# Attention values with the exp blocks as weights: V and a column of ones moving through TensorE, x turned back by transposes

## The chip, the cores and the metric

One NeuronCore of a Trainium2 chip runs the whole program. The metric is device time in microseconds (us), taken several times; the median counts. The profile is one further execution, with the start and end of every instruction. The engines are PE (TensorE; its weight loads are listed apart as PEld), ACT (ScalarE), DVE (VectorE), POOL (GpSimd) and SP, which only issues DMAs.

## The reference

Attention over 8 batches of 12 heads, 448 positions and 64 channels, with q and k normalised, and a two-layer product on its result:

```python
q_n, k_n = rmsnorm(q, g_q), rmsnorm(k, g_k)           # x / sqrt(mean(x*x) + 1e-6) * g
scores = matmul(q_n, k_n.T) / sqrt(64)                # per batch and head, 448 x 448
attn = exp(scores - max);  attn = attn / (sum(attn) + 1e-9)
x = matmul(attn, v)                                   # heads side by side: 3584 x 768
h = x @ w_in                                          # 768 -> 2048
g = h + sin(alpha * h)**2 / (alpha + 1e-9)
out = g @ w_out                                       # 2048 -> 768
```

The inputs are float32; matmul operands are bf16, sums are float32 in PSUM.

## The kernel before

**Stages.** The work goes batch by batch, in eight stages, b = 0 to 7. In stage b the kernel makes the attention of batch b (12 heads, in three groups c = 0, 1, 2 of four heads) and the first product of batch b. The second product of batch b-1 is cut into units of 64 matmuls and pushed in small steps of 8 matmuls between the attention's steps of stage b. After stage 7 the second product of batch 7 stands alone: the tail.

**The order is written out by hand.** Each stage has a string of tokens (`STAGE_0` for b = 0, `STAGE_1` for b = 1, `STAGE_N` for all later ones), which the program walks from left to right; each engine's queue holds what its tokens issued, in that order. A digit n stands for n steps `F` of the second product's oldest unit, `f` is a step of the next unit (`fill`, of lines L548 and L529). `S` is one tile of scores: four matmuls (L357) and one exp on ACT (L360) for four heads, 64 keys each, and 448 queries. `o`, `v`, `x`, `y`, `z` are parts of `attend`: the sums of the exps by matmuls with ones (L404, L416) and the values product (L416), with V as the weights and the exps moving. `q`, `u`, `r`, `g`, `k` are the normalisation of q and k: squares (L281 on POOL, L278 on ACT), their sums on DVE (L290), the inverse root on ACT (L299, L300), the product with g on POOL (L286) and the scaling (L309, on POOL, or on DVE in stage 0). `t` turns the result by a DMA transpose that SP issues (L319), `p` by TensorE (L334). `l`, `V`, `W`, `O` load q and k (SP), v, w_in and w_out (POOL).

**The values product before.** A tile of exps holds keys in partitions and queries along the row, so x comes out with channels in partitions, which is what the first product wants. The division is made in three ways on ACT and DVE: the sums' logarithm and exp(-ln) on ACT (L423 to L432), for group 0 folded by four reductions on DVE (L429), and then a product out of PSUM on DVE into xT (L440).

**The first product** (`first_product`, L468) has 96 matmuls of 128 x 128 weights and 448 columns a stage. Two matmuls' outputs share a PSUM pair; each pair goes through sin on ACT (L446), a square on POOL (L449) or ACT (L451) and a sum on DVE (L454) into g_sb. It starts on the groups of x that are ready.

**PSUM** is four slots of two banks. Which slot each step takes is a written string of digits too; a step waits until the last reader of its slot is done.

Of the kernel before, what the change touches and what calls it, by code (L numbers as in the profile page):

```python
# [17 lines left out]
try:  # L18
# [15 lines left out]
        "q000 u000 q010 G q011 q001 u010 g00 u011 r01 g01 D1 u001 k01 r00 k00 q11 u11 O00 q10 V00 p012 "  # L34
        "W01 q20 p00 g1 u10 r1 q21 u20 V01 g2 S4 V02 S k11 l3 k10 S1 S1 S4 W00 W02 S u21 r2 p1 L S2 S q31 "
        "S3 k21 q30 k20 D2 S S3 o3 l4 g3 S W10 W12 o1 o3 p2 u30 l5 S3 u31 S1 S W11 S4 v7 S S S q40 S S x5 "
        "y3 q41 u41 x1 g4 z4 u40 x1 r4 y4 O01 q50 z3 r3 O10 "
    ),
    "012311203203312021021302301231032103021321302",
    {-1: 'u50 O11 k30', 0: 'D4 k401', 1: 'k411', 2: 'q51', 3: 'k31 k400 u51', 5: 'k410', 7: 'g5 V12', 8: 't3 V10 V11 t4 l6 l7'},  # L40
# [3 lines left out]
        "4 r2 f f k20 1 f f 2 k21 S 1 q31 1 t2 S 1 S 2 S q30 2 S 2 S S 3 f S 3 S 1 f S 1 S 1 u31 2 l5 g3 "  # L44
        "S u30 o1 o6 1 r3 V10 2 S f q41 1 f 2 S 2 S 2 q40 S u41 1 v1 v1 S v3 V12 S k31 q50 v2 u40 S 2 S "
        "V11 g5 S z4 x7 y7 r4 z3 g4 k30 "
    ),
    "1320201203203013133213130101301231203123",
    {-1: 'u50 t3', 0: 'k41', 2: 'k40', 5: 'q51', 6: 'l6 t4', 8: 'u51 l7'},
# [3 lines left out]
        "f q40 f 1 f 2 q41 1 S 1 r2 5 f S f f S 2 S 1 u40 k20 1 k21 S 1 u41 1 S 2 S 1 q31 1 o7 1 f f 1 S "  # L53
        "t2 f 1 r4 S 2 f 1 l5 q30 S 3 S 1 u31 1 S 2 u30 g3 V10 S 2 S S k41 3 S v6 r3 k30 S k31 v1 S 2 V12 "
        "g4 2 S 2 S 2 q51 l6 S t3 z3 x7 y5 y2 z4 V11 "
    ),
    "01223131310312323203013012301021310231023",
    {-1: 'k40', 0: 't4', 2: 'q50', 3: 'u50', 4: 'u51 g5', 6: 'l7'},
)
LAST = "0123012"  # L60


def tokens_of(plan):

    return [t for word in plan.split() for t in ("F" * int(word) if word.isdigit() else [word])]
# [3 lines left out]
def kernel(  # L69
# [14 lines left out]

# [12 lines left out]
    NC = NP // 2  # L105
    SCALE = float(D) ** -0.5
# [8 lines left out]
    vpool = ctx.enter_context(tc.tile_pool(name="vpool", bufs=2))  # L115
    npool = ctx.enter_context(tc.tile_pool(name="norm", bufs=2))
    tpool = ctx.enter_context(tc.tile_pool(name="qkT", bufs=8))
    epool = ctx.enter_context(tc.tile_pool(name="expT", bufs=17))
    hpool = ctx.enter_context(tc.tile_pool(name="parts", bufs=1))
    rpool = ctx.enter_context(tc.tile_pool(name="rec", bufs=2))  # L120
    xpool = ctx.enter_context(tc.tile_pool(name="xT", bufs=1))
# [6 lines left out]

# [3 lines left out]
    upcoming = deque()  # L132
# [11 lines left out]
    qk, vb, norm = {}, {}, {}  # L144

    def strip(pp, hi):

        s = 2 * hi + pp
        return slice(s * 32, s * 32 + 32)

    def half_of(c, pp, hi):

        return pp ^ (hi, 1, 0)[c]

    def load_qk(ci, k_queue=nc.sync):

# [17 lines left out]
    def load_v(b, c):  # L174


        if b not in vb:
            vb[b] = vpool.tile([P, NP, NJ, D], BF16, tag="vb", name="vb")
        heads = v[b].rearrange("(n pp) (p j) d -> n pp p (j d)", pp=2, j=NJ)
        rows = vb[b].rearrange("p n j d -> p n (j d)")  # L180
        if c == 1:
            for r in range(2):
                nc.gpsimd.dma_start(out=rows[r * 64:r * 64 + 64, 1:4], in_=heads[1:4, 1 - r].rearrange("n p x -> p n x"))
        else:
            n = slice(0, 1) if c == 0 else slice(4, NP)
            nc.gpsimd.dma_start(out=rows[:, n], in_=heads[n].rearrange("n pp p x -> (pp p) n x"))
# [15 lines left out]
    ones = const.tile([P, D], BF16)  # L202
    nc.vector.memset(ones, 1.0)
    ones_row = const.tile([1, P], F32)
    nc.vector.memset(ones_row, 1.0)
    eps = const.tile([P, 1], F32)
# [13 lines left out]
    def spread_g():  # L220

        nc.gpsimd.tensor_mul(g_rows[:, 2], g_rows[:, 0], g_rows[:, 1])
        ps = bank_pair("gps")
        nc.tensor.matmul(ps[:, 0, :D], ones_row, g_rows[:, 2], start=True, stop=True)
        nc.vector.tensor_copy(gg[:, 0], ps[:, 0, :D])
        give_back(ps)

    def spread_alpha():

# [6 lines left out]
    def load_w_in(half, c):  # L236


        cols = slice(half * D_FF // 2, (half + 1) * D_FF // 2)
        rows = moe_w_in[c * 2 * P:(c + 1) * 2 * P, cols]  # L240
        nc.gpsimd.dma_start(out=w_in_sb[half][:, 2 * c:2 * c + 2],  # L241
                            in_=rows.rearrange("(p x) f -> p x f" if c else "(x p) f -> p x f", x=2))

    def load_w_out(hi, lo):
        src = moe_w_out.rearrange("(mt p) d -> p mt d", p=P)
        part = 2 * hi + lo
        mts = slice(part * MT // 4, (part + 1) * MT // 4)
        nc.gpsimd.dma_start(out=w_out_sb[:, mts], in_=src[:, mts])  # L248

    def keep_busy(n, rhs):  # L250


# [7 lines left out]
    def norm_tasks(ci):  # L260

        st = SimpleNamespace()
        early = ci <= NC
        st.ms = npool.tile([P, 2, 2 * NJ], F32, tag="ms", name="ms")
        st.inv, st.inv_ps, st.scaled = {}, [], 0
        st.sq, st.n = {}, None
# [5 lines left out]
        def square(w, heads=(0, 1)):  # L274
            if ci < 2:
                st.sq[w] = spare(2 * ci + w).rearrange("p (a d) -> p a d", d=D)
                rows = slice(heads[0] * NJ, (heads[-1] + 1) * NJ)
                nc.scalar.activation(st.sq[w][:, rows], qk[ci][:, w, rows], ACT.Square)  # L278
            else:
                st.sq[w] = npool.tile([P, 2 * NJ, D], F32, tag="sq", name="sq")  # L280
                nc.gpsimd.tensor_mul(st.sq[w], qk[ci][:, w], qk[ci][:, w])  # L281
# [10 lines left out]
        def rsqrt(ws=slice(0, 2)):  # L292
            ln = npool.tile([P, 2, 2 * NJ], F32, tag="inv", name="inv")
            inv = bank_pair("inv") if early else ln
            if early:
                st.inv_ps.append(inv)
            for w in range(2)[ws]:
                st.inv[w] = inv[:, w, :2 * NJ]
            nc.scalar.activation(ln[:, ws], st.ms[:, ws, :], ACT.Ln, scale=1.0 / D, bias=eps)  # L299
            nc.scalar.activation(inv[:, ws, :2 * NJ], ln[:, ws], ACT.Exp, scale=-0.5)  # L300

        def scale(w, heads=(0, 1)):
            eng = nc.vector if early else nc.gpsimd
# [20 lines left out]


# [22 lines left out]
    def scores(c, j, warm=0):  # L348

# [3 lines left out]
        for pp in range(2):  # L353
            for hi in range(2):
                qkt, r = qkT[2 * c + pp], slice(hi * 64, hi * 64 + 64)
                o = half_of(c % NC, pp, hi) * 64
                nc.tensor.matmul(sc[o:o + 64, hi, :S], qkt[r, 1, j * REST:(j + 1) * REST], qkt[r, 0, :],  # L357
# [5 lines left out]
    avs, recs = {}, {}  # L363
    presums = {}

    def add_tile(b):


        if b not in presums:
            presums[b] = SimpleNamespace(n=0, t=rpool.tile([P, 2, S], F32, tag="rec", name="rec"))  # L370
        s = presums[b]
        first = expT[b * NC, 0] if s.n == 0 else s.t
        s.n += 1
        nc.vector.tensor_add(s.t, first, expT[b * NC, s.n])

    def split_sum(b):

        s = presums[b]
        assert s.n == NJ - 1
        s.parts = [hpool.tile([P, 2, S], BF16, tag=f"part{i}", name="part") for i in range(2)]  # L380
        nc.vector.tensor_copy(s.parts[0], s.t)
        nc.vector.tensor_sub(s.parts[1], s.t, s.parts[0])
    STEPS = {"o": "ones 0", "v": "values 0", "x": "ones 1", "y": "low 1", "z": "high 1"}

    def attend(b, what, tiles=range(NJ)):

        kind, both = what.split()
        both = both == "1"  # L390
        if tiles[0] == 0:
            avs[what] = bank_pair("av")
        av = avs[what]
# [287 lines left out]
```

The softmax here doesn't subtract the row's maximum and nothing guards it: scores larger than these inputs give would overflow.

## Time and profile before

| what | value |
|---|---|
| time, median of 3 runs | 409.0 us (408.0 to 409.46) |
| span of the profiled execution, first to last instruction | 405.8 us |
| PE busy | 391.4 us (96%) |
| ACT busy | 315.3 us (78%) |
| POOL busy | 283.6 us (70%) |
| DVE busy | 240.6 us (59%) |
| granted TensorE clock | 0.999 of full |
| DMA, mean | 137 GB/s |

The page gives the span of the profiled execution and no other time of it; the median of the runs is 3.2 us longer than that span, which is what lies around it. The time in a row of a group is the union of its instructions' times; neighbouring matmuls overlap in the array, so a group's mean is longer than its share. "Idle before" is idle time of that engine, with what ended it.

### The profile page before, as it was taken

The numbers are of one execution on the slowest core, as the hardware profiler recorded it, in microseconds if no ns is written. First come the engines' busy times: TensorE is split into PE (matmuls) and PEld (weight loads), VectorE is DVE, ScalarE is ACT, GpSimd is POOL, SyncE is SP. The second block draws the span as 40 slices with busy tenths as digits, with TensorE's granted clock in tenths as the row PEclk, the third lists the DMA queues.
The fourth block names the chain that finished last, engine by engine and source line by source line (L and its number), as shares of the span: only waits on it lengthen the run. The fifth ranks groups of instructions, "written<-read, shape, count | busy, mean of one in ns | idle before, by whom it ended". The sixth has DMA issues, their size and how long they took to land.

```text
span 405.8 us, 15218 instructions
## 1 busy us (share of the span) xinstructions
PE 391.4 (96%) x6755; PEld 238.8 (59%) x6758; DVE 240.6 (59%) x364; ACT 315.3 (78%) x474; POOL 283.6 (70%) x268
## 2 busy tenths in 40 slices
PE   1999999999999999999999999999999999999996
PEld 1346467645675566755676556755667556765564
DVE  4956665756783576638584475836685485544512
ACT  5798889868896879958898678958898679877600
POOL 5998889987959789588877779597895784003300
PEclk9999999999999999999999999999999999999999
DMA  7999999855286925697076923879046901620022
GB/s 266 215 254 241 210 221 255 193 155 171 53 164 162 151 94 88 182 198 153 3 140 178 200 102 70 185 158 209 3 94 179 166 2 22 108 61 1 2 78 79
DMA packets 67846, 55.46 MB, mean 137 GB/s; under 512 B 41524, under 2 KB 63172, under 8 KB 67780
## 3 DMA queue, kind: packets, MB, share of 16 engines
q1 hardware_dynamic: 56578, 41.43, 42.2%
q0 software_dynamic: 10432, 11.81, 19.0%
q8 instruction: 53, 0.87, 0.9%
q10 hardware_dynamic: 770, 1.25, 0.9%
q14 instruction: 13, 0.11, 0.1%
HBM read 45.62 MB, written 11.01 MB: 140 GB/s over the span
## 4 chain that ended last, share of the span: by engine, by line
PE 88%; POOL 5%; DMA 3%; issue 1%; DVE 1%; ACT 1%; SPq 0%; POOLq 0%
PE hps L468 34%; PE ops L548 31%; PE av L416 9%; PE sc L357 7%; PE ops L529 5%; POOL sq L281 2%; DMA qk<-in_q_dram 2%; DMA qk<-in_k_dram 2%; PE av L404 1%; POOL qk L286 1%; POOL w_out_sb L248 1%; POOL w_in L241 1%; ACT expT L360 1%; DVE g_sb L454 0%; DVE xT L440 0%
## 5 line engine op out<-in xcount | busy, mean ns | idle before, releaser
L360 ACT ACTIVATE expT<-sc 128x896 bf16<-128x896 f32 x168 | 143.7, 917 | 7.4 <-PE sc L357 6.6
L548 PE MATMUL ops<-w_out_sb,g_sb 64*64 64x384 bf16 x3072 | 148.0, 323 | 0.0
L468 PE MATMUL hps<-xT,w_in 128*128 128x448 bf16 x768 | 147.0, 353 | 0.4 <-DVE g_sb L454 0.4
L468 PEld LDWEIGHTS <-w_in 128*128 128x128 bf16 x768 | 74.4, 98 | 72.5 <-issue 3.9
L454 DVE SCALAR_TENSOR_TENSOR g_sb<-s,inv_alpha_sb,hps 128x448 bf16<-128x448 f32 x128 | 81.1, 676 | 59.1 <-POOL s L449 58.5
L548 PEld LDWEIGHTS <-g_sb 64*64 64x64 bf16 x3072 | 91.9, 107 | 37.0 <-issue 3.8
L449 POOL TENSOR_TENSOR s<-s 128x448 f32<-128x448 f32 x64 | 59.6, 932 | 65.7 <-ACT s L446 43.9
L446 ACT ACTIVATE s<-hps,alpha_sb 128x448 f32<-128x448 f32 x128 | 73.9, 627 | 37.7 <-PE hps L468 37.2
L309 POOL TENSOR_TENSOR qkn<-qk,inv 128x448 bf16<-128x448 f32 x80 | 72.9, 938 | 24.6 <-issue 17.1
L281 POOL TENSOR_TENSOR sq<-qk 128x896 f32<-128x896 f32 x44 | 73.3, 1678 | 3.9 <-DVE ms L290 3.0
L357 PE MATMUL sc<-qkT 64*64 64x448 bf16 x672 | 60.3, 357 | 0.7 <-ACT expT L360 0.3
L286 POOL TENSOR_TENSOR qk<-qk,gg 128x896 f32<-128x896 f32 (+1 forms) x25 | 50.5, 2021 | 2.2 <-ACT g_sb L278 1.5
L554 DVE COPY osb<-ops 128x384 f32<-128x384 f32 x48 | 26.7, 556 | 38.5 <-PE ops L548 38.3
L290 DVE TENSOR_REDUCE ms<-sq 128x14 f32<-128x896 f32 x44 | 46.4, 1078 | 3.3 <-POOL sq L281 3.2
L440 DVE TENSOR_TENSOR xT<-av,rec 128x896 bf16<-128x896 f32 (+1 forms) x26 | 25.7, 1016 | 26.8 <-ACT rec L432 21.4
L451 ACT ACTIVATE s<-s 128x448 f32<-128x448 f32 x64 | 36.9, 577 | 2.9 <-DVE g_sb L454 0.7
L416 PE MATMUL av<-expT,vb 64*32 64x448 bf16 (+1 forms) x1120 | 38.1, 350 | 0.0
L357 PEld LDWEIGHTS <-qkT 64*64 64x64 bf16 x672 | 21.7, 107 | 13.8 <-issue 6.7
L555 DVE TENSOR_TENSOR osb<-osb,ops 128x384 f32<-128x384 f32 x48 | 26.6, 554 | 1.7
L416 PEld LDWEIGHTS <-vb 64*32 64x32 bf16 (+1 forms) x1120 | 20.8, 96 | 11.0 <-issue 2.2
L429 DVE TENSOR_REDUCE rec<-rec 32x448 f32<-32x448 f32 x28 | 17.1, 610 | 9.7 <-ACT rec L425 9.4
L529 PE MATMUL ops<-w_out_sb,g_sb 128*128 128x384 bf16 (+1 forms) x144 | 21.0, 309 | 0.0
(51 smaller groups left out, 185.8 us busy)
## 6 DMA issues: line engine op xcount, KB each, us to landing
qk<-in_q_dram SPq DMA_DIRECT2D x23, 448.0 KB, 5.2
qk<-in_k_dram SPq DMA_DIRECT2D x23, 448.0 KB, 5.7
out_dram<-osb SPq DMA_DIRECT2D x45, 192.0 KB, 2.9
w_out_sb<-in_moe_w_out_dram POOLq DMA_DIRECT2D x4, 768.0 KB, 12.8
w_in<-in_moe_w_in_dram POOLq DMA_DIRECT2D x6, 512.0 KB, 12.2
vb<-in_v_dram POOLq DMA_DIRECT2D x16, 168.0 KB, 7.2
vb<-in_v_dram POOLq DMA_DIRECT2D x8, 224.0 KB, 5.3
out_dram<-osb SPq DMA_DIRECT2D x13, 96.0 KB, 4.3
```

The source lines that it names most:

```text
L281: nc.gpsimd.tensor_mul(st.sq[w], qk[ci][:, w], qk[ci][:, w])
L286: nc.gpsimd.tensor_mul(x, x, gg.to_broadcast([P, len(heads) * NJ, D]))
L290: nc.vector.reduce_sum(st.ms[:, w, rows], st.sq[w][:, rows], axis=AX.X)
L309: eng.tensor_mul(n[:, :, hi, :], x[:, hi], inv[:, hi].unsqueeze(2).to_broadcast([P, NJ, D]))
L357: nc.tensor.matmul(sc[o:o + 64, hi, :S], qkt[r, 1, j * REST:(j + 1) * REST], qkt[r, 0, :], start=True, stop=True)
L360: nc.scalar.activation(expT[c, j], sc[:, :, :S], ACT.Exp, scale=SCALE)
L416: nc.tensor.matmul(av[o, k, :S], w, x[r, hi, :], start=(j == 0), stop=(j == last))
L446: nc.scalar.activation(s1, hps, ACT.Sin, scale=alpha_sb[:, m, :])
L449: nc.gpsimd.tensor_mul(s2, s1, s1)
L454: nc.vector.scalar_tensor_tensor(g_sb[:, m, (b % 2) * S:(b % 2 + 1) * S], s2, inv_alpha_sb[:, m, :], hps, op0=ALU.mult, op1=ALU.add)
L468: nc.tensor.matmul(ps[:, m % 2, :S], w_in_sb[m * 2 // MT][:, kt, m % (MT // 2) * P:(m % (MT // 2) + 1) * P], x[:, kt, :], start=(kt == ORD ...
L548: nc.tensor.matmul(st["ps"][os, r, :HALF], g_sb[rs, m, c0 + o * 64:c0 + o * 64 + 64], w_out_sb[rs, m, half * HALF:(half + 1) * HALF], star ...
```

## The change

V gets a column of ones, and swaps its place with the exps. A block of exps of 128 keys by 128 queries is the weights, and V's 64 channels with the ones (65 columns) move. Queries are now in the output's partitions, 65 columns for each block of 128 queries: 64 of x and one of the sum. The tiles of scores pair two key strips of one head in the 128 partitions; of the seven strips of 64 keys the last has no partner, and holds two heads. So for a group there are six paired tiles and one last one, and four heads of 448 queries give, in each paired tile, six blocks of 128 queries and two half blocks of 64, and in the last tile 28 quarter-array blocks.

DVE takes the reciprocal of the sums and multiplies (L378, L380); x then has queries in partitions, and is turned back: by a DMA transpose on SP (`T`, `turn`) or by seven matmuls and a copy (`P`, `pe_turn`: stage 0, and the last group of stage 1). V is loaded as float32 by SP, three loads a batch, and cast into v_pair and v_last by POOL (`c`) or DVE (`C`). Some squares move from POOL to ACT (`Q`), and the scaling after `R` is on POOL. The first product is opened early: `H` runs, for two outputs, the four of six steps that need only groups 0 and 1, inside the token string. The token strings and the slots are written anew; batch 0's second product takes all left halves first, each stored by itself.

```diff
 STAGE_N = (
     (
-        "f q40 f 1 f 2 q41 1 S 1 r2 5 f S f f S 2 S 1 u40 k20 1 k21 S 1 u41 1 S 2 S 1 q31 1 o7 1 f f 1 S "
-        "t2 f 1 r4 S 2 f 1 l5 q30 S 3 S 1 u31 1 S 2 u30 g3 V10 S 2 S S k41 3 S v6 r3 k30 S k31 v1 S 2 V12 "
-        "g4 2 S 2 S 2 q51 l6 S t3 z3 x7 y5 y2 z4 V11 "
+        "3 q40 S 1 g4 f 2 f f S 2 S 2 S u40 3 S R2 V10 2 S q30 1 S 2 S 2 q41 V11 S k20 1 v6 v1 S f f S f f S "
+        "S f S k21 V12 u41 f t2 f 1 f 1 R4 u30 T0 k41 l5 2 S 1 S S k40 3 v6 Q31 S v1 2 S 2 S 2 u31 Q50 f 1 S "
+        "v7 r3 f f c12 g3 T1 f f f T2 3 H u50 k30 Q51 g5 k31 H C10 C11 u51 l7 t3 l6 t4 "
     ),
...
-    epool = ctx.enter_context(tc.tile_pool(name="expT", bufs=17))
+    epool = ctx.enter_context(tc.tile_pool(name="expT", bufs=14))
...
+    def load_v(b, part):
+        if b not in vs:
+            vs[b] = [vpool.tile([P, H, NK, D], F32, tag="vs", name="vs"), vpool.tile([P, NP, D], F32, tag="vl", name="vl")]
+        if part < 2:
+            rows = v[b].rearrange("h (p j) d -> p h j d", j=NJ)[:, :, part * NK:(part + 1) * NK]
+            nc.sync.dma_start(out=vs[b][0][part * 64:part * 64 + 64], in_=rows)
         else:
-            n = slice(0, 1) if c == 0 else slice(4, NP)
-            nc.gpsimd.dma_start(out=rows[:, n], in_=heads[n].rearrange("n pp p x -> (pp p) n x"))
+            rows = v[b].rearrange("(n pp) (p j) d -> pp p n j d", pp=2, j=NJ)[:, :, :, NJ - 1]
+            nc.sync.dma_start(out=vs[b][1], in_=rows.rearrange("pp p n d -> (pp p) n d"))
+
+    def cast_v(b, c, eng):
+        heads = slice(4 * c, 4 * c + 4)
+        eng.tensor_copy(v_pair[b % 2][:, heads, :, :D].rearrange("p h j d -> p (h j) d"),
+                        vs[b][0][:, heads].rearrange("p h j d -> p (h j) d"))
+        eng.tensor_copy(v_last[b % 2][:, 2 * c:2 * c + 2, :D], vs[b][1][:, 2 * c:2 * c + 2])
...
+    def values(b, c, js):
+        if js[0] == 0:
+            avs[b, c] = bank_pair("av")
+        av = avs[b, c]
+        es = {j: expT.pop((b * NC + c, j)).rearrange("p hi s -> p (hi s)") for j in js}
+        for whole in (True, False):
+            for j in js:
+                if j == NJ - 1:
+                    continue
+                pp, k = divmod(j, NK)
+                for i in range(NJ):
+                    if (i == NJ // 2) == whole:
+                        continue
+                    for o in range(1 if whole else 2):
+                        hi = o if i == NJ // 2 else i // (NJ // 2 + 1)
+                        n = P if whole else 64
+                        q0 = i * P + o * 64
+                        nc.tensor.matmul(av[o * 64:o * 64 + n, pp, i * W:(i + 1) * W], es[j][:, q0:q0 + n],
+                                         v_pair[b % 2][:, 4 * c + 2 * hi + pp, k], start=(k == 0 and i == 0), stop=False)
+        if js[-1] < NJ - 1:
             return
+        for i in range(NJ):
+            for o in range(2):
+                pos = 2 * i + o
                 for pp in range(2):
...
+                    r = slice(pp * 64, pp * 64 + 64)
+                    nc.tensor.matmul(av[o * 64:o * 64 + 64, pp, i * W:(i + 1) * W], es[NJ - 1][r, pos * 64:pos * 64 + 64],
+                                     v_last[b % 2][r, 2 * c + pos // NJ], start=False, stop=(i == NJ - 1))
+        sums = av[:, :, :NJ * W].rearrange("p pp (i w) -> p pp i w", w=W)
+        rec = npool.tile([P, 2, NJ, 1], F32, tag="rec", name="rec")
+        nc.vector.reciprocal(rec, sums[:, :, :, D:])
+        xn[b, c] = npool.tile([P, NJ, 2, D], BF16, tag="xn", name="xn")
+        nc.vector.tensor_mul(xn[b, c].rearrange("p i pp d -> p pp i d"), sums[:, :, :, :D], rec.to_broadcast([P, 2, NJ, D]))
+        give_back(avs.pop((b, c)))
+
+    def turn(b, c):
+        x = xT[b, c] = xpool.tile([P, 2, S], BF16, tag="xT", name="xT")
+        nc.sync.dma_start_transpose(out=x.rearrange("p k s -> p (k s)").rearrange("p (i t) -> p i t", t=P),
+                                    in_=xn.pop((b, c)).rearrange("p i pp d -> p (i pp d)"))
+
+    def pe_turn(b, c, act):
+        tp = bank_pair("xt", BF16)
+        src = xn.pop((b, c))
+        for i in range(NJ):
+            nc.tensor.transpose(tp[:, 0, i * P:(i + 1) * P], src[:, i].rearrange("p pp d -> p (pp d)"), ident)
+        x = xT[b, c] = xpool.tile([P, 2, S], BF16, tag="xT", name="xT")
+        out = x.rearrange("p k s -> p (k s)")
+        if act:
+            nc.scalar.copy(out, tp[:, 0, :2 * S])
         else:
...
+            nc.vector.tensor_copy(out, tp[:, 0, :2 * S])
+        give_back(tp)
...
+    def open_product(b):
+        i = len(opened)
+        opened[i] = bank_pair("hps")
+        for m in (2 * i, 2 * i + 1):
+            multiply(b, i, m, range(KT - 2))
```

`multiply` issues the first product's matmuls of one output (128 of the 2048 columns) for the given steps kt; `first_product` closes the opened outputs with the two steps of group 2 and goes on with the others. The end of stage 0's new string, which the prediction walks, is this:

```text
... q31 q30 v7 S S1 W12 u31 D4 S4 O00 l5 P10 S1 S1 u30 r3 g3 S1 V11 Q50 k31 Q51 H g4 O01 O10 k30 v7 H P20 p3 L O11 g5 ...
```

## The prediction

> **What bounds the kernel now.** First the page's busy times and slices, then the stretches (us; each engine's busy time and instructions, in the order PE, PEld, DVE, ACT, POOL):
>
> ```profile
> PE 391.4 (96%) x6755; PEld 238.8 (59%) x6758; DVE 240.6 (59%) x364; ACT 315.3 (78%) x474; POOL 283.6 (70%) x268
> ...
> PE   1999999999999999999999999999999999999996
> ```
>
> ```profile
> 26.00:40.00 14.00, 13.32 (x257) 7.67 (x257) 9.24 (x13) 12.06 (x20) 13.14 (x11) 1.00 1.12 239
> ...
> 147.20:194.10 46.90, 46.90 (x888) 29.34 (x884) 29.21 (x44) 38.78 (x59) 36.87 (x33) 1.00 0.63 135
> ```
>
> PE is never idle in a late stage, and the next engine (ACT) has 8 us to spare. A busy PE need not be full, so I read the chain of waits, which gives what each piece adds (start, us, count). Of one late stage:
>
> ```profile
> 109.86 0.80 PE av L404 x56
> ...
> 119.64 1.14 PE av L416 x24
> ...
> 120.97 0.19 PE av L416 x4
> ...
> 124.51 4.10 PE av L416 x168
> 128.61 18.27 PE hps L468 x96
> ```
>
> The stages repeat every 46.92 us ((381.47 - 99.96)/6, between the ends of the hps pieces). The pieces sum to that: hps 18.27; 448 ops matmuls in fours of 0.1625 (16 take 0.65) 18.2; 21 tiles of scores at 0.19, 4.0; sums and values 0.80 + 1.14 + 0.19 + 4.10 = 6.23; together 46.7. So a late stage is PE work alone, and the change is worth what it does to the **6.23 us**. Stage 0 (to 54.42) differs: ACT (12.06 of 14) and POOL (13.14 of 14) are as full as PE, and DMA is saturated. Stage 1 ends at 99.96, the tail is 24.3 us.
>
> [...]the 128-column load takes 98 ns, the 64-column one 107. [...]q and k's transposes, 128-column weights with 64 columns moving:
>
> ```profile
> 17.52 0.77 PEld L334 LDWEIGHTS <-qkn 64*128 64x128 bf16 x28 [0.36 <-issue]
> 17.52 0.89 PE L334 MATMUL tp<-ident,qkn 64*128 64x64 bf16 x28
> ```
>
> Starts spread over 0.89 - 0.19 (one matmul) = 0.70 us, 26 ns a pair; within one row half the starts are 29 ns apart: the load hides wholly. These use 64 rows; the last units of the tail load all 128, and 16 pairs of 192 columns take 1.32 us, 82 ns each, which is 80 of columns and 2 more. [...]The trace measured far more from issue to landing (us), so I use the trace:
>
> ```profile
> DMA to landing us min/median/max: 3.1/4.8/10.5
> ```
>
> **The change, part by part; first a late stage.**
> Removed: the 6.23 us of PE.
> Added on PE, per group and three times a stage:
> - 36 whole-array pairs, 108 a stage. 448 columns take 190.3 ns (18.27/96), 192 take 82.5: slope 0.42 ns, so 65 take 29; 29.5 with a ns for margin: 3.2 us. [...]
> - 12 half-width pairs, 36 a stage, in twos on different columns. 18 x 30 ns side by side, or 18 x 57 with loads in line (64 columns cost 107 against 93 ns for 32, so 64 columns stream in about 28): 0.54 to 1.03, I take 0.75. The four quarter loads of the ops already overlap.
> - 28 quarter pairs, 84 a stage, in fours on different quadrants: 21 x 30 to 57 ns, 0.63 to 1.2; I take 0.85.
> - Nine changes of shape. The trace has one: the last ones matmul to the next ops starts 186 ns later, where the block's pitch is 96: 90 lost. Between 0 and 90 each, 0.45 taken.
> Sum 5.25 (4.4 to 6.6) for 6.23: **-1.0 us a late stage**. Scores, ops and hps keep their counts; their order changes nothing in the sum.
>
> What must stay hidden. (1) x of group 2. After `v7`: 8 steps of ops (64 matmuls, 2.6 us) and two `H` (16 x 0.19 = 3.04) need nothing of group 2: cover 5.64. Behind it: the reciprocal (0.25, by the 128x16 row), the product out of PSUM (1.09, by L440's row), 0.1 for semaphores, then `T2` on SP. The median 4.8 includes loads alongside; pairs without landed after 3.9 to 4.9 (109.5 and 156.6), the best after 3.1. With 4.5 the chain is 5.95: PE waits 0.3 (0 to 5). (2) The scores tile just before `v7`: its exp starts up to 0.8 late behind the square of `Q50` and takes 0.9; the whole and half blocks ahead of it last 1.3: 0.2 (0 to 0.4). Net **-0.5**, six stages: -3.
>
> Other engines there. ACT loses the Ln and Exp (three of 0.56, two of 0.93: 3.5) and gains three squares of 0.94: -0.7. POOL loses three squares of 1.68 and four V loads of 0.67, gains a cast of 1 to 1.6: -6. DVE loses four reductions of 0.61 and three products, gains three products, three reciprocals and two casts of 0.5 to 1: about 0. All are under PE's 46; worth nothing, covered by PE. The cast `c12` waits on POOL for V's loads, issued 10 us ahead, with `g3` and `k30` queued behind it and `t3` behind those: nothing needs them before the next stage's scores. SP gains three loads of about 0.5 and three transposes of 1.3 a stage. `T1` and `T2` stand behind two stores of a unit done before group 1's `v6`, so they don't wait for them; behind `T2` are only stores and next loads. V's last strip goes in 256-byte pieces; DMA share is 0.63 there, so slower pieces are hidden. Fourteen exp tiles in place of 17 cost nothing: walking the string, at most 11 are alive, before group 1's `v6`.
>
> **Stage 1**: before, 45.54 against a sum of 44.1 (64 ops matmuls fewer). After, 43.1, and 0.9 for the group turned by PE behind ACT's copy (0.94) and a first wait for exps: 44.0, -1.5 (-2.5 to 0).
>
> **Stage 0.** From the first exp (13.9) to the last (33.8) ACT was full: 21 exps at 0.83 = 17.4, and 1.9 of Ln and Exp for group 0, which go. The first score comes 0.3 later (q of the first pair scaled on POOL, two of 0.94). So scores end near 31.5. Then on PE: `H` 1.5, `v7` 1.7, `H` 1.5, turning 0.2, 28 transposes 0.8 (DVE's copy of x beside them), 80 of L468 15.2: 52.4, against 54.42. w_in's last part is issued behind four squares on POOL, near 34 (before: 29.1, landed 43.6), and V moves as float32 beside it; its matmuls come at 44. I charge 0.5: **-1.5** (-3 to +4). w_out's right half (`O10`, `O11`) goes out near 40 and took 12 to 17 us before, so it is there by 57; with batch 0's left halves first, its first use is three units (24 steps, at least 7.8 us) after stage 1's start, 60.
> The **tail** has the same units: 0.
>
> Sum: -3.0 - 1.5 - 1.5 = -6.0. Against the profiled execution the span is 405.8 - 6.0 = 399.8; with the 3.2 us of the median around it, **403.0**.
>
> **Rivals.**
> - A, loads not hidden (slower): [...]It decides from 37 ns a pair (6.0/(7 x 108) = 8 ns over 29.5). [...]against: the 29 ns and the 82 ns above. 0.1.
> - B, x comes late: `T2` lands like the transposes beside loads (6 to 7 us after issue): PE waits 2 more in six stages, +12: 415. From 5.5 us it eats the gain. For: landings to 10.5 in this trace; against: no load is issued within some 8 us before it. 0.15.
> - C, ACT binds: the scores come in bursts, exps take 0.9 each, and ACT is busy 25 of the attention's 27.5 us. What PE saves returns as waits for exps: about 408. Against: the exps lag at most 1.4 us when I walk the string, and three or more slots serve scores in those stretches. 0.1.
> - D, halves and quarters overlap fully, no waits: 5.25 falls to 4.4 and the 0.5 of waits go: 1.35 x 7 = 9.5 more, 393.5. 0.15.
> - E, the likeliest, 0.5: 403, own range 399 to 407.
>
> **How the numbers follow.** A measurement of this kernel tells about 0.3% (1.2 us) from no change. E and D are faster, and some of C: 0.67; the rest of C and the edge of B the same: 0.08; A, B and a bad stage 0: 0.25. From 393 to 414 leaves out A, the lower third of D and the upper third of B, 0.2.
>
> **What would show it.** Right: the new whole-array group 29 to 31 ns apart in the timeline; the values pieces of a late stage summing to 4.8 to 5.8; the distance between hps ends 46.3 to 46.6; stage 0's hps ending near 53. Wrong: 50 ns or more between starts (A); PE's hps waiting for the DMA of xT by more than 1 us (B); PE's scores or av waiting for ACT by over 1 us a stage (C); w_in's landing after 46 with hps waiting for it (stage 0's step).

## The result and the profile after

The kernel after takes **448.8 us** (median of 4 runs, 444.8 to 451.4) where the kernel before took 409.1 beside it: ratio 1.097 [1.091, 1.104]. It is slower, where the prediction had it 1.5% faster. The profiled execution took 451.4 us, the longest of the four; its span is 449.3 us against 405.8, and the stretches below are cut from that span. (Time and span of one execution differ by 1.7 to 2.1 us in all runs below; of the 3.2 us that the prediction adds to the span, about 1 is the spread among executions.) None of the runs below is faster than the kernel before; the nearest takes 415.7 us where that one takes 407.2.

From the page of the kernel after (busy us, share, instructions; then tenths of 40 slices, of PE and of the clock that PE was granted):

```profile
PE 401.6 (89%) x6637; PEld 252.9 (56%) x6637; DVE 246.6 (55%) x390; ACT 305.1 (68%) x454; POOL 242.9 (54%) x240
...
PE   1899199889989999699996999889996999999996
...
PEclk9999779999998999889998999989998899999999
```

PE is no longer full, and it is busy for 10.2 us longer although it has less to do: at the later 1 and at the sixes of its row, or just behind them, the clock is lower too. Cut at the ends of the first products (us), the stages are these; the differences add up to 43.5, which is the whole difference of the spans:

| | stage 0 | stage 1 | stages 2-6, mean | stage 7 | tail |
|---|---|---|---|---|---|
| before | 54.3 | 45.5 | 46.9 | 46.9 | 24.5 |
| after | 67.3 | 49.6 | 52.3 | **46.5** | 24.6 |
| difference | +13.0 | +4.1 | +26.7 for five | -0.45 | +0.1 |

Stage 7 is the only one with the new products and no load of a further batch. It is as long as was forecast for all late stages. The stretches of stage 3 and stage 7 of the kernel after (stretch, length, then busy time and instructions of PE, PEld, DVE, ACT, POOL, then clock, DMA share, GB/s):

```profile
168.15:221.26 53.11, 49.27 (x857) 31.27 (x856) 29.31 (x47) 37.84 (x56) 30.38 (x28) 0.94 0.66 145
378.25:424.72 46.47, 46.47 (x857) 30.06 (x857) 21.89 (x37) 34.53 (x49) 11.09 (x12) 1.00 0.30 57
```

The same 857 PE instructions take 46.47 and 53.11 us. 3.84 of the difference is idle time, 2.80 is busy time at a lower clock. What PE waits for in stage 3 (total, times, longest), and the chain of waits there (start, us, what):

```profile
PE sc L339 <- DMA qkT<-qkn: 3.8, 1, 3.8
```

```profile
177.10 3.63 POOL qkn L294 x4
...
180.75 8.00 DMA qkT<-qkn
...
188.79 0.59 PE sc L339 x4
189.38 0.64 PE ops L508 x8
...
192.69 2.30 PE av L365 x48
...
198.69 1.52 PE av L365 x47
```

The scores of the stage's last group wait for the DMA transpose `t2` of q and k. After the wait one step of ops (8 matmuls) takes 0.64 us instead of 0.33, and a block of the values product 2.30 instead of 1.52. The granted clock there, and in a like stretch of stage 2:

```profile
187.57:188.79 1.22, 0.00 (x0) 0.00 (x0) 0.00 (x0) 0.00 (x0) 1.22 (x3) 0.50 1.07 239
188.79:194.40 5.61, 5.61 (x77) 3.60 (x78) 1.11 (x2) 3.48 (x4) 2.97 (x3) 0.50 0.77 212
...
136.37:139.78 3.41, 3.41 (x48) 3.10 (x44) 0.00 (x0) 2.16 (x3) 3.41 (x5) 0.50 0.94 138
```

In stage 3, 2.6 us after PE had gone idle (at 184.95), the clock fell to 0.50 and stayed there for 6.83 us, the last 5.61 of them with PE at work. In stage 2 it fell 0.6 us after the end of a wait of 2.74 us and stayed for 3.41.

Why `t2` is late is seen in SP's queue in that stage (start, us until the issue is done, DMA):

```profile
177.00 1.87 SPq L167 DMA_DIRECT2D vs<-in_v_dram  x2
178.91 0.65 SPq L170 DMA_DIRECT2D vl<-in_v_dram  x1
180.75 5.99 SPq L304 DMA_TRANSPOSE qkT<-qkn  x2
```

V's three loads stand just ahead. The two issues of `t2` take 5.99 us (4.18 and 1.71), where the kernel before needs 2.67 for them in its stage 3 (from 146.7):

```profile
156.63 2.67 SPq L319 DMA_TRANSPOSE qkT<-qkn  x2
```

In the kernel after, the first half lands 8.0 us after its start, 20.6 after the stage's start. PE was ready for it at 16.8. In the kernel before it starts at 9.9 and lands at 14.7, and PE comes to those scores at 18.3. So the new order alone, without V, starts `t2` 2.7 us later and needs it 1.5 us sooner.

In stage 0 the waits are others (total, times, longest):

```profile
PE hps L424 <- DVE g_sb L412: 9.2, 1, 9.2
ACT sq L263 <- DMA qk<-in_q_dram: 7.8, 1, 7.8
...
DVE v_last L176 <- DMA vl<-in_v_dram: 3.5, 1, 3.5
```

The cast `C10` of batch 1's V stands in DVE's queue ahead of the g_sb of the first outputs, and V's last load, issued at 27.3, lands at 53.9. So the first product waits 9.2 us for data that stage 0 does not use. Beside it ACT waits 7.8 for q, whose load `l5` stands on SP behind V's `V10`.

### The profile page after: what moved, and what is told of

It reads as the page before. It is cut to its first block, busy times and chain, and to the rows that moved or that the text cites. A ratio compares the mean times of both kernels' runs of the same rounds, so it can differ in the third digit from the quotient of the medians.

```text
span 449.3 us, 15061 instructions
## 1 busy us (share of the span) xinstructions
PE 401.6 (89%) x6637; PEld 252.9 (56%) x6637; DVE 246.6 (55%) x390; ACT 305.1 (68%) x454; POOL 242.9 (54%) x240
## 4 chain that ended last, share of the span: by engine, by line
PE 52%; DMA 20%; POOL 12%; DVE 8%; issue 3%; ACT 3%; SPq 0%; ACTq 0%; POOLq 0%; DVEq 0%
PE hps L424 21%; PE ops L508 17%; DMA qkT<-qkn 8%; DMA vl<-in_v_dram 6%; PE av L365 6%; DVE g_sb L412 5%; PE sc L339 5%; POOL s L407 4%; PE ops L491 3%; DMA qk<-in_k_dram 3%; POOL qkn L294 3%; POOL sq L265 3%; POOL qk L270 2%; DMA vs<-in_v_dram 1%; PE av L374 1%
## 5 line engine op out<-in xcount | busy, mean ns | idle before, releaser
L508 PE MATMUL ops<-w_out_sb,g_sb 64*64 64x384 bf16 x3072 | 156.4, 332 | 4.4 <-issue 4.4
L424 PE MATMUL hps<-xT,w_in 128*128 128x448 bf16 x768 | 150.6, 357 | 9.9 <-DVE g_sb L412 9.9
L508 PEld LDWEIGHTS <-g_sb 64*64 64x64 bf16 x3072 | 95.7, 110 | 41.3 <-issue 9.9
L407 POOL TENSOR_TENSOR s<-s 128x448 f32<-128x448 f32 x64 | 60.4, 944 | 94.4 <-ACT s L404 51.1
L412 DVE SCALAR_TENSOR_TENSOR g_sb<-s,inv_alpha_sb,hps 128x448 bf16<-128x448 f32 x128 | 81.3, 678 | 49.9 <-POOL s L407 49.9
L339 PE MATMUL sc<-qkT 64*64 64x448 bf16 x672 | 63.1, 379 | 17.7 <-DMA qkT<-qkn 16.1
L515 DVE COPY osb<-ops 128x384 f32<-128x384 f32 x48 | 26.7, 556 | 78.2 <-PE ops L508 75.7
L274 DVE TENSOR_REDUCE ms<-sq 128x14 f32<-128x896 f32 x44 | 47.1, 1077 | 6.3 <-ACT sq L263 5.0
L339 PEld LDWEIGHTS <-qkT 64*64 64x64 bf16 x672 | 23.1, 110 | 33.9 <-DMA qkT<-qkn 18.3
L365 PEld LDWEIGHTS <-expT 128*128 128x128 bf16 (+1 forms) x1152 | 36.5, 103 | 9.9 <-issue 7.5
L365 PE MATMUL av<-v_pair,expT 128*128 128x65 bf16 (+1 forms) x1152 | 40.4, 199 | 0.3 <-POOL v_pair L174 0.3
L265 POOL TENSOR_TENSOR sq<-qk 128x896 f32<-128x896 f32 x23 | 38.3, 1680 | 3.6 <-DMA qk<-in_q_dram 1.7
L380 DVE TENSOR_TENSOR xn<-av,rec 128x896 bf16<-128x896 f32 x24 | 26.2, 1091 | 0.8
L263 ACT ACTIVATE sq<-qk 128x896 f32<-128x896 f32 x21 | 19.7, 943 | 9.9 <-DMA qk<-in_q_dram 7.8
L378 DVE RECIPROCAL rec<-av 128x14 f32<-128x14 f32 x24 | 5.9, 245 | 32.0 <-PE av L374 32.0
```

Of the source, the lines that this page charges most:

```text
L265: nc.gpsimd.tensor_mul(st.sq[w][:, rows], x, x)
L274: nc.vector.reduce_sum(st.ms[:, w, rows], st.sq[w][:, rows], axis=AX.X)
L339: nc.tensor.matmul(sc[o * 64:o * 64 + 64, hi, :S], qkt[r, 1, key * REST:(key + 1) * REST], qkt[r, 0, :], start=True, stop=True)
L365: nc.tensor.matmul(av[o * 64:o * 64 + n, pp, i * W:(i + 1) * W], es[j][:, q0:q0 + n], v_pair[b % 2][:, 4 * c + 2 * hi + pp, k], start=(k = ...
L407: nc.gpsimd.tensor_mul(s2, s1, s1)
L412: nc.vector.scalar_tensor_tensor(g_sb[:, m, (b % 2) * S:(b % 2 + 1) * S], s2, inv_alpha_sb[:, m, :], hps, op0=ALU.mult, op1=ALU.add)
```

## The experiments

Theory at the start: V's loads and casts, put where they delay something else, are the whole loss. Rivals: the order of the normalisation on POOL makes `t2` late; the loads overload the DMA wherever they stand; the new order as such is bad. Stage lengths of all runs, in us; the ratio is to the kernel before on the same chip, with its 95% interval:

| run | stage 0 | stage 1 | 2-6, mean | stage 7 | median | ratio |
|---|---|---|---|---|---|---|
| after | 67.3 | 49.6 | 52.3 | 46.5 | 448.8 | 1.097 [1.091, 1.104] |
| e1_v_after_t2 | 67.7 | 50.9 | 53.8 | 46.5 | 459.5 | 1.126 [1.122, 1.130] |
| e2_k2_first | 66.2 | 51.7 | 55.1 | 46.9 | 464.6 | 1.138 [1.130, 1.147] |
| e3_casts_late | 62.0 | 50.9 | 51.6 | 46.5 | 444.1 | 1.088 [1.085, 1.091] |
| e4_both | 61.4 | 50.5 | 55.3 | 46.9 | 460.6 | 1.127 [1.124, 1.131] |
| e5_v_once | 57.5 | 49.2 | 47.0 | 46.5 | 417.0 | 1.023 [1.009, 1.037] |
| e6_v_pool_f32 | 76.3 | 52.7 | 51.7 | 46.6 | 460.3 | 1.129 [1.118, 1.140] |
| e7_v_wide | 58.9 | 49.9 | 48.9 | 46.5 | 426.4 | 1.046 [1.036, 1.055] |
| e8_v_pool_bf16 | 81.8 | 51.3 | 50.2 | 46.5 | 456.7 | 1.120 [1.110, 1.131] |
| e9_v_first | 67.0 | 50.0 | 46.6 | 46.5 | 423.4 | 1.039 [1.036, 1.042] |
| e10_first_late | 56.3 | 57.0 | 47.1 | 46.5 | 422.4 | 1.036 [1.034, 1.038] |
| e11_regrouped | 56.6 | 55.2 | 47.1 | 46.6 | 422.0 | 1.038 [1.032, 1.043] |
| e12_regroup_only | 62.6 | 51.3 | 51.1 | 46.5 | 442.9 | 1.087 [1.083, 1.090] |
| e13_t2_up | 55.4 | 51.1 | 47.3 | 46.5 | 415.7 | 1.020 [1.015, 1.025] |
| e14_t2_up_regrouped | 56.0 | 51.7 | 47.1 | 46.5 | 415.7 | 1.020 [1.017, 1.023] |
| e15_before_plus | 53.3 | 46.7 | 48.4 | 46.9 | 416.8 | 1.023 [1.018, 1.029] |

### V's loads behind t2

```diff
-"... u40 3 S R2 V10 2 S q30 1 S 2 S 2 q41 V11 S k20 ... k21 V12 u41 f t2 f 1 ..."
+"... u40 3 S R2 2 S q30 1 S 2 S 2 q41 S k20 ... k21 u41 f t2 V10 V11 V12 f 1 ..."
```

> In stages 2 to 7 the three V loads of the next batch are issued behind group 2's q and k transposes (t2) instead of ahead of them; t2's own start, set by POOL, stays. Theory 1 (V's loads, ahead of t2 in SP's queue and on the DMA engines, make it late): t2's first transpose goes back from 8.0 us to about 4.8 from issue to landing, PE's wait for group 2's scores (3.8 us, and slow-clock matmuls after it) shrinks to 0.5 to 1, stages 2 to 6 go from 52.3 to about 49, total 431 to 437. Theory 2 (POOL reaches k20 and k21 too late, after three squares and a product with g): most of the wait stays, total 443 to 449. Theory 3 (V as float32 is simply too much for the DMA engines, wherever it is put): the wait moves to another transpose, total 445 to 452.

A miss: slower by another 10 us. The wait of the scores for qkT is gone from most stages, and another is there. ACT's wait, SP's queue and the chain in stage 3 of this run:

```profile
ACT sq L263 <- DMA qk<-in_q_dram: 6.0, 1, 6.0
```

```profile
192.15 4.64 SPq L385 DMA_TRANSPOSE xT<-xn  x1
```

```profile
196.89 5.08 DMA qk<-in_q_dram
```

Now x's transpose `T0` is the DMA behind V: it takes 4.64 us to issue, and the load `l5` behind it starts at 196.9 and lands at 202.0. `Q31` on ACT waits for that q, with the exps of the next scores behind it, and PE waits 5.8 us for an exp. The delay moved one place down the queue.

### The scaling of group 2 first

```diff
-"3 q40 S 1 g4 f 2 f f S 2 S 2 S u40 3 S R2 V10 2 S ... S k20 ... k21 V12 u41 f t2 f 1 ..."
+"R2 3 S 1 k20 k21 q40 g4 f 2 f f S 2 S 2 S u40 3 S t2 V10 2 S ... S ... V12 u41 f f 1 ..."
```

> In stages 2 to 7 the inverse root of group 2 (R2) and its scaling (k20, k21) come first on ACT and POOL, and t2 stands ahead of the V loads on SP. Theory 1 and 2 together (t2 late by POOL's order and by V ahead of it): t2 is issued about 6 us after the first product's end instead of 12.6 and lands 5 us later, long before its scores; stages 2 to 6 go from 52.3 to 46.5 to 47, total 419 to 424. Theory 3 (too much DMA wherever it is put): V now collides with x's transposes and PE waits for xT; gain under 10 us, total over 438.

A miss too, slower by 16 us. The scaling was done at 180.0, 7.5 us after the stage's start, but `t2` was issued at 185.1, 12.6 after the start as in the kernel after. Waits of stage 3:

```profile
DVE ms L274 <- POOL sq L265: 3.7, 1, 3.7
...
PE sc L339 <- DVE osb L516: 3.2, 1, 3.2
```

DVE's sum `u40` waits for a square that now stands behind the scaling on POOL; the copy of a second product's output to SBUF (osb) stands behind `u40`; the store of that osb stands ahead of `t2` on SP, where it is issued at 183.9; and PE waits for the PSUM slot that the copy would free. V's loads, behind `t2` here, make `T0` take 4.92 us to issue as in the run before. So the order on POOL is not free to change, and this run says nothing for the rival of the late scaling.

### Stage 0's casts last

```diff
-        "C10 k411 "
+        "k411 "
...
-        1: "c11",
...
-        8: "C12 l6 l7",
+        8: "C10 C11 C12 l6 l7",
```

> In stage 0 the three casts of batch 1's V go behind the last of the first product's DVE and POOL work; nothing else moves. Theory (the casts stand in DVE's and POOL's queues ahead of g_sb's sums and wait for V's last load, landed at 53.85): PE's 9.2 us wait in the first product goes, stage 0 ends at 56 to 59 instead of 67.3, total 437 to 441. Rival (DMA is saturated, and the weights hold stage 0 anyway): w_in or w_out stops PE next, stage 0 and the start of stage 1 lose most of it again, total over 444.

Stage 0 gets 5.3 us shorter, half of what was expected. Its wait for g_sb falls from 9.2:

```profile
PE hps L423 <- DVE g_sb L411: 3.6, 1, 3.6
```

ACT still waits 6.8 us for the q load behind `V10`; a later run that moves `V10` behind that load too (e10) brings the stage from 62.0 to 56.3. This run with the one before:

> The edits of the two kernels before this one together (k20, k21 and t2 first in stages 2 to 7, stage 0's casts late). If both losses are queues' order and independent, the savings add up: 449 - 27 - 10 = 412, between 408 and 416; stage 1 keeps its 49.6. If DMA volume is what costs (theory 3), over 430.

A miss (412 was expected), since the second edit loses time: but the two add, stage 0 as here, stages 2 to 6 as there.

### V loaded once

```diff
     def load_v(b, part):
+        if b:
+            vs[b] = vs[0]
+            return
         if b not in vs:
```

> Control, with part of the computation left out: V is loaded for batch 0 alone (three loads), and every later batch casts and uses batch 0's V again; all casts, products, transposes and the order of everything else stay as in the kernel after. Theory 1 (V's loads, as small float32 pieces on SP's queue, cost something wherever they stand: the qk transpose t2 behind them, or the q/k loads behind them): with them gone stages 2 to 6 fall from 51.2-53.1 us to the 46.5 us of stage 7, which loads nothing (6 x 5.5 = 33 us less), stage 1 by some 3 us, and stage 0 by the 9.2 us that hps waits for V's cast: about 404 us (400 to 410). Theory 2 (the written order of POOL's squares and scalings and the casts make t2 late; V's loads add only the slow issue): t2 still starts some 2.5 us later after the stage's start than before, so stages of about 49 us and a total of 420 to 430 us. Theory 3 (V's loads don't matter): 440 us or more.

What this kernel leaves out is V of batches 1 to 7: it uses batch 0's throughout. It takes 417.0 us, in none of the three bands, but the stages tell the theories apart. Stages 2 to 6 are within 1 us of stage 7, as theory 1 has it. (Its sum counts six such stages where five have loads.) Stage 1 doesn't fall: 49.2 against 49.6, so V's loads are not what holds it. Two stretches:

```profile
106.68:153.15 46.47, 46.47 (x857) 30.02 (x856) 29.33 (x47) 37.73 (x56) 30.39 (x28) 1.00 0.62 136
153.15:200.48 47.33, 46.81 (x857) 30.14 (x856) 29.05 (x47) 37.74 (x56) 30.39 (x28) 1.00 0.64 133
```

The order, the casts, POOL's work and the products are all there, and PE is full. `t2` starts at the same 12.6 us, so the new order as such costs these stages little (0.5 us on the mean); but its first half now lands at 16.1, only 0.5 to 0.7 ahead of PE's need, where the kernel before has 3.6. V's loads cost stages 2 to 6 some 5.2 us each, and stage 0 9.9.

### The other queue

```diff
-            nc.sync.dma_start(out=vs[b][0][part * 64:part * 64 + 64], in_=rows)
+            (nc.gpsimd if b else nc.sync).dma_start(out=vs[b][0][part * 64:part * 64 + 64], in_=rows)
```

(and the same for `vl`.)

> V of batches 1 to 7 is loaded by POOL's queue instead of SP's, at the same places in the order, the same float32 tiles and the same pieces of 768 and 256 bytes. Theory 1a (the place ahead in SP's queue is what costs; the bytes and pieces do not): the transposes and q/k loads of SP no longer stand behind V, late stages of 47 to 48 us, total 410 to 420 us. Theory 1b (the DMA engines are what is overloaded by the small pieces, whichever queue gives them out): t2 still lands 8 us after issue, total 435 to 450 us. A cost on POOL itself (issues of about 1 us each, three in a stage, ahead of k20 and k21) would show as t2 starting 1 to 3 us later: then 420 to 430 us.

A miss, in no band: 460.3. POOL in stage 3 of this run (start, us):

```profile
186.12 0.79 POOL L167 DMA_DIRECT2D vs<-in_v_dram  x1
186.92 3.32 POOL L265 TENSOR_TENSOR sq<-qk 128x896 f32<-128x896 f32 x2
190.18 0.78 POOL L167 DMA_DIRECT2D vs<-in_v_dram  x1
190.96 3.62 POOL L294 TENSOR_TENSOR qkn<-qk,inv 128x448 bf16<-128x448 f32 x4
```

Two issues of 0.8 us stand ahead of the scaling, so `t2` starts 14.1 us after the stage's start instead of 12.6, and with V in flight it still lands 6.1 us after issue, at 20.3 (3.5 after issue without V, in e5). So another queue did not take V out of the transpose's way here, and the issue time was on the wrong engine. In stage 0 the loads stand behind w_in and w_out on POOL, and hps waits 17.6 us for the cast. With a cast to bf16 on the way it is hardly better (456.7, in no band either), and stage 0 is worse (81.8):

> All of V is loaded by POOL's queue and cast to bfloat16 on the way, as in the kernel before, but into the pieces that the kernel after needs; the casts become copies from bfloat16 to bfloat16. Theory 1a: like the run with float32 on POOL's queue or a few us better, 405 to 420 us, since SP's queue holds only q, k, transposes and stores. Theory 1b: 435 to 450 us. In stage 0 the loads of V compete on POOL with w_in and w_out: if that costs, stage 0 stays above 60 us.

### Larger pieces

```diff
...
+        if b:
+            rows = v[b].rearrange("(n pp) (p j) d -> pp p n (j d)", pp=2, j=NJ)[:, :, 2 * part:2 * part + 2]
+            nc.sync.dma_start(out=vs[b][2][:, 2 * part:2 * part + 2], in_=rows.rearrange("pp p n x -> (pp p) n x"))
+            return
```

> V of batches 1 to 7 is loaded by SP at the same places, with the same bytes in three loads, but in pieces of 1792 bytes over 128 partitions (whole rows of seven 64-float keys); the data then lie in another order in the tile, so the casts and the values product work on wrongly placed keys: the arrangement of V is what this kernel leaves out. Everything else is as in the kernel after. Theory 1b (small pieces are what makes V's loads slow): the three loads land in 4 to 6 us instead of 6.7 to 9, t2 is issued and lands as before, late stages 47 to 49 us, total 412 to 428 us. Theory 1a (the queue position alone): within 5 us of the kernel after, 440 to 450 us.

426.4, in the band of theory 1b. What this kernel leaves out is V's right arrangement. With the same bytes, places and queue, 768 pieces of 1792 bytes instead of 2304 of 768 and 256 take 3.4 of the 5.2 us off each of stages 2 to 6, and 8.5 off stage 0. `t2` is still not as before: its two issues take 3.1 to 5.5 us. And the pieces are not the only thing that changed: each load now spreads over 128 partitions, where two of the three covered 64. No run takes the two apart. From the pages of the kernel after and of this run (DMA, queue, count, KB each, median us to landing):

```profile
vs<-in_v_dram SPq DMA_DIRECT2D x16, 576.0 KB, 7.9
...
vl<-in_v_dram SPq DMA_DIRECT2D x8, 192.0 KB, 9.0
```

```profile
vs<-in_v_dram SPq DMA_DIRECT2D x21, 448.0 KB, 5.5
```

### V's loads given out first

```diff
-"3 q40 S 1 g4 f 2 f f S 2 S 2 S u40 3 S R2 V10 2 S q30 1 S 2 S 2 q41 V11 S k20 ... k21 V12 u41 f t2 ..."
+"V10 V11 V12 3 q40 S 1 g4 f 2 f f S 2 S 2 S u40 3 S R2 2 S q30 1 S 2 S 2 q41 S k20 ... k21 u41 f t2 ..."
```

> One edit to the kernel after: in stages 2 to 7 V's three loads (V10 V11 V12) are given out first of all, some 9 us earlier, where SP's queue holds nothing else and no transpose follows for 12 us. Theory A (V's loads cost only through the qk transpose t2 that stands right behind them: its issue takes 4.2 us instead of about 1.3 and its first half lands 20.6 us after the stage's start instead of 16): t2 lands at about 16 us, the 3.8 us wait of the scores goes, stages 2 to 6 fall from 52.3 to about 47 us: 449 - 5 x 5.2 = 423 us (419 to 428). Theory B (V's small pieces load the DMA engines so that something else waits wherever V stands, as in the two runs that moved them behind t2): 440 us or more.

A hit: 423.4. A stretch of this run:

```profile
163.50:209.97 46.47, 46.47 (x857) 30.05 (x856) 29.31 (x47) 37.74 (x56) 30.40 (x28) 1.00 0.75 165
```

SP gives the loads out while the first product still runs, and they have landed 4.9 us after the stage's start, long before `t2` is due at 12.6. The small pieces, the float32 and SP's queue are all as in the kernel after; five of the six late stages are now as short as stage 7. So it isn't too many bytes for the DMA engines: it is what stands right behind these pieces. `t2` in stages 2 to 6 of the runs, in us (the landing is that of its first half, where the trace has it):

| run | starts after the stage's start | two issues | landing after its start |
|---|---|---|---|
| before | 9.7-10.3 | 2.7-3.8 | 4.4-4.9 |
| after | 12.6 | 5.9-6.4 | 7.1-8.2 |
| e5, no V | 12.6 | 2.9-4.0 | 3.3-3.5 |
| e6, V on POOL's queue | 14.1 | 3.1-3.7 | 5.7-6.1 |
| e7, larger pieces | 12.6 | 3.1-5.5 | 5.0-6.9 |
| e9, V first | 12.6 | 2.9-3.9 | 3.3-3.5 |

### Stages 0 and 1

```diff
 STAGE_0
-"... S1 p2 V10 S W11 ... O00 l5 P10 ... C10 k411 "
+"... S1 p2 S W11 ... O00 l5 V10 P10 ... k411 "      # and 8: "C10 C11 C12 l6 l7"
 STAGE_1
-"f f f f f 1 f S R2 1 f k20 f k21 S ... v6 v1 V10 S S ... T1 1 V11 u40 ... R4 f V12 f S ..."
+"V10 V11 V12 f f f f f 1 f S R2 1 f k20 f k21 S ... v6 v1 S S ... T1 1 u40 ... R4 f f S ..."
```

> The edit of the run with V first, and the same in stage 1, and in stage 0 V's first load behind the q/k load l5 and all three casts after the last hps product. Theory A: as that run, less the 9.2 us that hps waited for V's cast in stage 0 and the 7 us that ACT waited for the q/k load: stage 0 at 57 to 59 us as in the run without V's loads, stage 1 at 47 to 50, stages 2 to 7 at 47: 412 us (408 to 418). Theory B: 435 us or more. The kernel before is reached only if nothing of the order of stages 0 and 1 costs.

Half a hit: stage 0 falls to 56.3, but stage 1 grows to 57.0. PE's longest wait there, and SP's queue (V's loads, then stores and `t2`):

```profile
PE sc L338 <- DMA qkT<-qkn: 8.4, 1, 8.4
```

```profile
66.92 1.32 SPq L166 DMA_DIRECT2D vs<-in_v_dram  x2
68.34 1.28 SPq L169 DMA_DIRECT2D vl<-in_v_dram  x1
69.73 6.21 SPq L477 DMA_DIRECT2D out_dram<-osb  x4
76.04 2.96 SPq L303 DMA_TRANSPOSE qkT<-qkn  x2
```

In stage 1 the place at the front is not free: four q and k loads stand there (62.7 to 66.8), V's loads go behind them, and four stores and `t2` behind those. The four stores take 6.21 us to issue, the first of them 3.15 where a store at the end of this stretch takes 0.6, so not only transposes are held. The keys grouped otherwise, in that kernel and alone:

```diff
-            pp, key = (o, NJ - 1) if j == NJ - 1 else (j // NK, j % NK + NK * o)
+            pp, key = (o, NK) if j == NJ - 1 else (j // NK, j % NK + (NK + 1) * o)
```

(with loads of keys 0-3 and 4-6, or 0-2 and 3-6, of each head, and the casts to match.)

> The run before this one, and the keys are grouped otherwise: pairs are keys k and k + 4, the single key block is 3, so that each head's 64 rows are read as one piece of 1024 and one of 768 bytes: 1536 pieces per batch instead of 2304, [...]the same bytes, four loads, one small cast more per group. If the number of pieces sets V's DMA time: 2 to 6 us less than the run with the old pieces, most in stage 0 where the DMA engines are full: 406 to 412 us. If only the place counts: the same within 1 us.

> Only the grouping of the keys is changed against the kernel after (1536 pieces of 768 and 1024 bytes per batch instead of 2304 of 768 and 256, same bytes), all loads and casts where they were. If small pieces make t2's issue and landing slow: between the kernel after (449 us) and the run with 1792-byte pieces (426 us): 430 to 440 us. If bytes or places alone count: 445 us or more.

Alone it gives 442.9 (1.087 against 1.097), 3 us short of the expected band, and `t2`'s two issues still take 5.4 to 6.0 us: a third fewer pieces help little. With V's loads first it gives nothing that can be measured (422.0 against 422.4; 406 to 412 was expected). The last edit in stage 1 puts V's loads back where the kernel after has them and moves `t2`:

```diff
-"f f f f f 1 f S R2 1 f k20 f k21 S 2 S 2 S 2 S 2 S 1 S t2 2 S ..."
+"f f f f f 1 f S R2 1 f k20 f k21 t2 S 2 S 2 S 2 S 2 S 1 S 2 S ..."
```

> Stages 2 to 7 with V's loads first, stage 0 with V's first load behind the q/k load and the casts last (both as in the run with first and late), stage 1 with V's loads where the kernel after has them, and with one edit: the qk transpose t2 follows the scaling k21 at once, ahead of the output stores that stood before it on SP's queue. If t2's place in SP's queue is what holds stage 1: the 2 to 8 us wait of the scores for qkT goes, stage 1 takes 46.5 to 48.5 us, and the sum is 56.3 + 47.5 + 6 x 46.7 + 25 = 409 us (407 to 413). If loads and casts hold it in another way: stage 1 stays at 50 us or more, 412 to 422 us.

> The run before this one with the keys grouped so that V comes in 1536 pieces of 768 and 1024 bytes per batch instead of 2304 of 768 and 256. If nothing waits for V any more, its piece size doesn't matter: within 1.5 us of that run. If V still delays something: 2 us less or more.

415.7 for both, not 409: the piece size no longer matters, and stage 1 stays at 51.1. PE's longest wait in stage 1 of the first, and the stretch:

```profile
PE sc L338 <- DMA qkT<-qkn: 2.8, 1, 2.8
```

```profile
55.40:106.48 51.08, 46.56 (x800) 29.14 (x799) 33.14 (x53) 37.68 (x56) 32.92 (x29) 0.97 1.14 231
```

`t2` is issued at 67.0 and its first half lands 6.8 us later, with no load of V right ahead of it: four q and k loads and two stores stand there. That these hold it as V did in the later stages fits the trace, but no run moves them. DMA share is 1.14 in this stage. Moving `t2` alone was not enough, and what a full repair of stage 1 would give was not tried. Of the 8.9 us between this span and that of the kernel before, 5.6 are in stage 1.

### V's small pieces in the kernel before

```diff
-"... S 2 S 1 u40 k20 1 k21 ..."
+"... S 2 S 1 u40 Y k20 1 k21 ..."      # Y: two loads of 6 heads' 768-byte pieces, one of all 256-byte pieces, on SP
```

> The kernel before, unchanged but for three loads more in each of stages 2 to 6 on SP's queue ahead of the qk transpose t2: small pieces of the next batch's V as the kernel after loads them (768 of 768 bytes and 768 of 256 bytes, two thirds of the pieces, 0.49 MB, for which there is room), into tiles that nothing reads. If V's small pieces ahead of t2 are by themselves the cause: t2's issue grows from 1.3 towards 3 us or more, its landing is 2 to 4 us later, stages 2 to 6 grow by 1 to 4 us each: 413 to 430 us. If only the new kernel's order and products make them dear: within 3 us of the kernel before.

A hit: 416.8, ratio 1.023 [1.018, 1.029]. These loads alone, read by nothing, cost the kernel before 1.5 us on the mean in each of the five stages. SP's queue in stage 3:

```profile
159.25 1.36 SPq L179 DMA_DIRECT2D more_vs<-in_v_dram  x2
160.65 0.71 SPq L181 DMA_DIRECT2D more_vl<-in_v_dram  x1
161.48 4.55 SPq L328 DMA_TRANSPOSE qkT<-qkn  x2
```

Two things add up: `t2` starts 2 us later, behind the issues of the loads, and its own issues take 4.55 us instead of 2.67. The effect per stage is smaller than in the kernel after. A third of the pieces is missing, `t2` still starts earlier (11.9) and is needed later (18.3), and after PE's longest wait for qkT, 2.4 us, the clock stays (0.999 over the whole run). How much each of these does was not taken apart.

## Why the prediction was wrong, point by point

- **The values product**: right, a little too good. Its pieces in stage 7 are three of 1.52 us (36 whole and 12 half blocks) and 0.35, 0.22 and 0.34 for the quarters: 5.47, against 5.25 forecast and 6.23 before. The whole blocks start 31 ns apart, and 29 was the estimate for their columns alone, so the loads hide but for some 2 ns: rival A falls. (The range of 4.4 to 6.6 doesn't come out of its terms: the upper ends add up to 6.2 with the whole pairs at 29.5 ns.)
- **x of group 2 and the exp before it**: forecast 0.5 of waits, none seen in stage 7. Rival B falls in its place, but its mechanism, a DMA transpose that lands late beside loads, came true for another transpose, `t2`. C falls: ACT is busy for 305.1 us, 10.2 less than before, and in stage 7 PE never waits for it. Of D, the missing waits came true, the 4.4 us did not.
- **The distance of the hps ends**, 46.3 to 46.6 forecast: 46.47 in stage 7 and in most late stages where V is out of the way. The match is in part luck. The values product gave 0.76 instead of 1.0, and the tiles of scores take 4.4 in stage 7's chain instead of 4.0; the 0.5 of waits that was charged and didn't come makes up for both.
- **The step that failed**: "DMA share is 0.63 there, so slower pieces are hidden", with "SP gains three loads of about 0.5". The share is a mean, and that small pieces are slower was the author's estimate (e7 fits it: 5.5 us to landing against 7.9 and 9.0). The three loads were costed by the time of their own issue, not by what stands right behind them. No step asked how much later than before `t2` starts (12.6 against about 9.7 us) and how much slack that leaves (0.5 to 0.7 us even without V, against 3.6). That is 5.2 us in each of five stages. e5 shows it by leaving V out, e9 by moving it, e15 by adding loads like it to the other kernel. Why SP's issues take longer behind such loads stays open. Of the 43.5 us, these runs put some 26 in stages 2 to 6 and 11 in stage 0 down to V's loads and casts; most of stage 1's 4.1 and the rest of stage 0 stay unexplained.
- **The order "changes nothing in the sum"**: nearly true of the sum (the scores' 0.4), not of the waits. And waits are paid again in clock: in stages 2 to 6 PE is idle 17.4 us and busy 11.5 longer than five times 46.47.
- **Stage 0**: forecast 52.9, measured 67.3. The +4 allowed for w_in was the wrong risk. The cast `C10` was not followed into DVE's queue, where it stands ahead of g_sb and waits for a load that took 26.5 us. e10 shows 11 us of the stage to hang on the places of V's loads and casts. The other 2.5 to 3.4 us, by which it stays above the forecast in e13 and e10, were not taken apart.
- **Stage 1**: forecast 44.0. PE is busy for 45.1 us there, 0.1 less than before, so the forecast gain of 1.5 wasn't in the work. The rest is waits, the longest for `t2` (1.9). e5 has much the same without V (1.5 for `t2`, 49.2 in all), so they are not V's doing; their cause stays open.
- **The tail**: forecast 0, measured 0.1.

## What to carry to other kernels

A load that nothing waits for can still hold what stands behind it in its queue (e15: `t2`'s issues take 4.55 us instead of 2.67): name the next DMA, when it starts, when its result is needed, and what is left between the two. The shape of a load can count as well as its bytes (e7: 48.9 us a stage instead of 52.3 with the same bytes), and here it did best where the queue was empty for its whole landing time (e9: 46.6). A cast of data that is still coming belongs behind everything that is due on its engine (e3: hps waits 3.6 us instead of 9.2); here stages 2 to 6 were repaired by moving three tokens, which changes no engine's sum of work. The gain that the change itself can have is small beside this: 0.45 us a late stage, seen only in stages that wait for nothing.

## What the runs showed of the hardware that was not expected

- The time of an issue on SP was no constant: two halves of a qk transpose took 2.67 us in the kernel before and 5.99 behind V's loads; of four plain stores behind them (e10), the first took 3.15 and the last 0.59.
- Another queue did not separate the two transfers: V on POOL's queue left the transpose on SP at 6.1 us to landing (e6, stage 3), where it takes 3.5 without V (e5).
- 48 pairs of a weight load (128 rows; 36 of 128 columns, 12 of 64) and 65 moving columns take 1.52 us, 32 ns each (stage 7 of the kernel after).
- After PE's wait of 3.84 us eight matmuls of ops took 0.64 us instead of 0.33. No one length of wait decides: the clock fell to 0.50 after 2.74 us (stage 2 of the kernel after) and was 0.97 on the mean of stage 1 of e13, whose longest wait is 2.8; it stayed up after 1.9 (stage 1 of the kernel after, 1.00) and 2.4 (e15, 0.999). In stage 3 of e2, with waits of 3.2 and 2.6, PE is idle for 7.7 of 55.0 us and so busy for 47.3, 0.8 over the 46.47 at full clock, where stage 2 of the kernel after with its 3.41 us at a half is busy for 48.48.
